# New places for all steps of a fused attention and feed-forward kernel, with a recalibrated planner

## The chip, the cores and the metric

The kernel runs on one core of a Trainium2 chip. The metric is the device time of one execution in microseconds, the median of several runs, lower is better. The engines are called as the profile calls them: PE is TensorE's matrix multiplication (PEld its weight loads), DVE is VectorE, ACT is ScalarE, POOL is GpSimd, and SP is SyncE, which here does nothing but issue transfers.

## The reference

Two stages, all in float32. The first is a linear recurrence for 4 batches and 8 heads over 768 time steps with head size 48; the second is a two-layer network on its output (3072 rows of 384 values, 2048 hidden).

```python
for t in range(S):
    cur = einsum('bhd,bhe->bhde', u * k[t], v[t])
    y[t] = einsum('bhd,bhde->bhe', r[t], state + cur)
    state = w[t][..., None] * state + einsum('bhd,bhe->bhde', k[t], v[t])
x = y.transpose(0, 2, 1, 3).reshape(B * S, H * D)
out = maximum(x @ w_in, 0) ** 2 @ w_out
```

## The kernel before, in words

**The work.** Time is cut into 6 chunks of 128 steps. For a chunk c and a batch b the *attention unit* (called A0.1 below for chunk 0, batch 1) loads r, k, w and v, turns r, k and w so that head and feature lie on the partitions, forms running products of w with a scan on DVE (L603, steps `scan`), scales r and k by them (`rt`, `rk`, `kn`), multiplies them on PE (`mt`, `mix`, L768 to L786), masks on DVE and writes the transposed output x, split into a high and a low part, as the operand of the network (`x`, L830). The recurrence's state goes from chunk to chunk: `dS` on PE (L760) is the new outer product, `S` on DVE (L847) adds it.

The network of a chunk (F0.5 is chunk 0, block 5 of 128 hidden units; 16 blocks) is `hp` on PE (nine matrix products, L869), squared ReLU and a split into two parts on ACT and DVE (steps `g`, L874 to L881), and `ob` on PE (three products for each of three output tiles, L888; L914 in the last chunk). Each product in float32 is made of three with split operands. The first blocks of chunk 0 (6) and of chunk 1 (8) are done in two halves, a for batches 0 and 1, b for batches 2 and 3, so that the network can start when half of the chunk's attention is there; after that every block takes 512 columns.

**Slices.** For chunk 0 the turning is done on PE (`turn`, L588). For later chunks it is done in two steps: DVE transposes 32 by 32 blocks (`z`, L542, two for a pair of batches), then 16 transfers that SP issues (`pt`, L552; 48 or 96 KB each, in pieces of 32 values) put the blocks into their places. The first scan of the chunk (L603) needs all 16. For the pair A1.0 and A1.1, SP can issue the first of them only when both `z` have ended.

**Weights.** W0 to W7 are the eight groups of both weight matrices. Of each, SP loads seven pieces: six of w_in (L468; 112 rows are 224 KB, 48 rows 96 KB, 32 rows 64 KB) and one of w_out (L470, 768 KB). Each half is then split into a high and a low part by ACT (widen, L487, and L507), three operations on DVE (L491, L495, L500) and one on POOL (L508). W3's pieces are wanted by block 6 of chunk 0, which comes after the halves.

**Order.** Every engine executes its instructions in order, and the order is written out by hand. Each step is registered with `P.add(engine, cost, rank, fn, ...)`, where rank is the next number of its row in the table `Places.PLACE`; `Plan.order` sorts each engine's steps by that number, so the numbers alone give the order on each engine. The planner then simulates the program with the costs given to `P.add` and the latencies `LAT`; from its times come three things only: the order in which the code of different engines is emitted, which buffer of a pool a step gets, and how many filler transposes PE executes while it waits (`P.filler`, L966: ten at the start, and up to as many as fit into a planned wait before 110 us). Steps marked `port` use a path to memory that DVE and POOL share, and the planner lets only one of them run at a time:

```python
t, news = max(s.ready, free.get(unit, 0.0), free.get("port", 0.0) if s.port else 0.0), {}
...
return None if s.todo or t == float("inf") else (t, unit)
...
at, unit = min(x for x in (start(u) for u, l in todo.items() if l) if x)
```

So among steps of several engines with one planned time the engine's name decides.

Of the kernel before, what the change touches and what calls it, by code (L numbers as in the profile page):

```python
# [9 lines left out]
F32 = mybir.dt.float32  # L10
# [4 lines left out]
AF = mybir.ActivationFunctionType  # L15
# [16 lines left out]
class Plan:  # L32
# [7 lines left out]
    LAT = {"pe": 0.2, "act": 0.1, "dve": 0.1, "pool": 0.1}  # L40
# [35 lines left out]
    def order(self):  # L76
# [89 lines left out]
class Places:  # L166
    PLACE = {
        "un": (39, 102, 107,),
        "load": (1, 3, 6, 2, 8, 11, 26, 19, 30, 34, 67, 86, 122, 136, 79, 340, 297, 317, 505, 499, 504, 707, 694, 700, 920, 906, 914, 1080, 1069, 1075, 1227, 1225, 1230, 1399,
# [4 lines left out]
        "turn": (9, 47, 50, 24, 29, 13, 35, 42, 65, 73, 78, 109, 113, 127,),  # L174
        "scan": (20, 16, 15, 18, 32, 28, 25, 27, 90, 72, 91, 87, 137, 124, 138, 123, 302, 326, 304, 329, 338, 324, 341, 342, 663, 598, 658, 656, 595, 590, 604, 586, 704, 762,
# [9 lines left out]
        "beta": (53, 59, 56, 61, 97, 103, 153, 177, 250, 357, 460, 447, 687, 685, 870, 863, 1074, 1063, 1162, 1161, 1304, 1336, 1494, 1489, 1680, 1617, 1809, 1859,),  # L185
        "flip": (251, 358, 461, 448, 670, 626, 879, 854, 1086, 1070, 1184, 1178, 1391, 1342, 1484, 1453, 1701, 1677, 1860, 1878,),
# [898 lines left out]
```

## Time and profile before

| | |
|---|---|
| time, median of 3 runs | 523.11 us (521.79 to 523.46) |
| the profiled execution: its own time | 520.64 us |
| its span, first to last instruction | 518.8 us |
| granted TensorE clock, mean | 0.995 of full speed |
| PE busy | 508.5 us (98%) |
| DVE, ACT, POOL busy | 361.5, 278.0, 106.6 us |

The trace is that of one execution. The time holds some 1.8 us around the span. L-numbers are lines of the kernel; "ob<-g,wo" means that the operation writes tile ob from tiles g and wo, and a bracket at the end of a timeline row is the idle time of that engine before it and what ended it.

### The profile page before, as it was taken

Reading aid. Unit: us, or ns where it says so; the run is one execution under the profiler, and the core shown is the slowest. Engines: PE = TensorE matmul, PEld = TensorE weight load, DVE = VectorE, ACT = ScalarE, POOL = GpSimd, SP = SyncE. Lnnn points to the kernel's source line nnn. Section 1 sums busy time; section 2 is a strip of 40 time slices with the busy share of each in tenths; the row PEclk is TensorE's granted clock in tenths of the full one; section 3 lists DMA queues with packets and bytes.
Section 4 is the critical chain, followed back from the end, with each engine's and each line's share of the span. In section 5 each row is a group of like instructions: output and inputs, shape, how many; then the busy total and the mean of one; then the engine's idle time right before and its main releaser. Section 6 shows DMA issues by size and latency. Waiting matters only on the chain.

```text
span 518.8 us, 12672 instructions
## 1 busy us (share of the span) xinstructions
PE 508.5 (98%) x4957; PEld 435.4 (84%) x4957; DVE 361.5 (70%) x723; ACT 278.0 (54%) x686; POOL 106.6 (21%) x141
## 2 busy tenths in 40 slices
PE   8999899999999999999999999999999999999996
PEld 7889798778999988888878788888888888889986
DVE  5999699998986878787878794846782342253323
ACT  4457679768936567636557354454562263223222
POOL 2355546235220413031050400220000000000000
PEclk9999989999999999999999999999999999999999
DMA  6899999776556566766646454345405001020001
GB/s 183 229 219 204 193 219 206 146 171 98 114 92 111 100 96 138 113 120 99 122 71 110 90 83 86 69 79 88 91 3 123 2 1 42 1 58 5 0 2 64
DMA packets 209186, 52.40 MB, mean 101 GB/s; under 512 B 200033, under 2 KB 204002, under 8 KB 209122
## 3 DMA queue, kind: packets, MB, share of 16 engines
q1 hardware_dynamic: 208802, 51.15, 51.8%
q8 instruction: 40, 0.66, 0.5%
q10 hardware_dynamic: 320, 0.40, 0.2%
q14 instruction: 24, 0.20, 0.1%
HBM read 33.03 MB, written 4.72 MB: 73 GB/s over the span
## 4 chain that ended last, share of the span: by engine, by line
PE 79%; SPq 14%; DMA 4%; issue 1%; DVE 1%; ACT 1%; DVEq 0%; ACTq 0%
PE ob L888 29%; PE a L869 20%; PE hp L869 13%; SPq L468 6%; PE ob L914 5%; SPq L552 4%; DMA ri<-in_moe_w_in_dram 2%; SPq L527 2%; PE a L786 2%; PE a L712 2%; PE hp L914 2%; PE a L753 1%; DMA pt<-st 1%; PE hp L786 1%; PE hp L712 1%
## 5 line engine op out<-in xcount | busy, mean ns | idle before, releaser
L888 PE MATMUL ob<-g,wo 128*128 128x512 f32 (+1 forms) x846 | 188.7, 365 | 2.7 <-DVE g L881 2.7
L888 PEld LDWEIGHTS ob<-g,wo 128*128 128x128 f32 x846 | 142.2, 190 | 27.7 <-DVE g L881 3.3
L869 PE MATMUL a<-x,wi 128*128 128x512 f32 (+1 forms) x594 | 132.6, 369 | 0.0
L869 PEld LDWEIGHTS a<-x,wi 128*128 128x128 f32 x594 | 103.0, 191 | 17.8 <-ACT g L880 0.2
L869 PE MATMUL hp<-x,wi 128*128 128x512 f32 (+1 forms) x396 | 86.3, 364 | 0.1
L869 PEld LDWEIGHTS hp<-x,wi 128*128 128x128 f32 x396 | 67.6, 189 | 12.3 <-DVE x L830 0.3
L874 ACT ACTIVATE t<-a 128x512 f32<-128x512 f32 (+1 forms) x66 | 36.0, 545 | 75.9 <-PE ob L888 34.1
L878 DVE SCALAR_TENSOR_TENSOR a<-a,t 128x512 f32<-128x512 f32 (+1 forms) x53 | 34.1, 643 | 52.4 <-ACT t L874 52.2
L874 ACT ACTIVATE t<-hp 128x512 f32<-128x512 f32 (+1 forms) x44 | 23.6, 537 | 54.2 <-PE hp L869 37.3
L881 DVE TENSOR_TENSOR g<-a,g 128x512 fp32r<-128x512 f32 (+1 forms) x66 | 40.7, 618 | 16.6 <-ACT g L880 16.1
L880 ACT CAST g<-a 128x512 fp32r<-128x512 f32 (+1 forms) x66 | 35.0, 532 | 28.8 <-DVE a L878 28.6
L878 DVE SCALAR_TENSOR_TENSOR hp<-hp,t 128x512 f32<-128x512 f32 (+1 forms) x35 | 22.6, 646 | 33.7 <-ACT t L874 33.5
L689 ACT ACTIVATE m<-near,beta 128x64 f32<-128x64 f32 x160 | 41.9, 338 | 2.4 <-PE hp L786 2.1
L603 DVE TENSOR_TENSOR_SCAN pt<-pt,zero 112x128 f32<-112x128 f32 x80 | 31.5, 422 | 10.6 <-DMA ri<-in_moe_w_in_dram 4.4
L632 POOL TENSOR_TENSOR st<-st 128x384 f32<-128x384 f32 x20 | 22.3, 1119 | 56.0 <-DVE st L542 53.9
L880 ACT CAST g<-hp 128x512 fp32r<-128x512 f32 (+1 forms) x44 | 23.1, 525 | 14.6 <-DVE hp L878 14.4
L881 DVE TENSOR_TENSOR g<-hp,g 128x512 fp32r<-128x512 f32 (+1 forms) x44 | 26.6, 605 | 4.1 <-ACT g L880 3.7
L914 PE MATMUL ob<-wo,g 128*128 128x384 f32 x144 | 28.7, 336 | 0.0
L542 DVE STREAM_TRANSPOSE st<-st 128x1152 f32<-128x1152 f32 x20 | 26.5, 1353 | 0.3 <-DMA st<-in_r_dram 0.3
L914 PEld LDWEIGHTS ob<-wo,g 128*128 128x128 f32 x144 | 25.6, 188 | 0.8
L634 POOL TENSOR_TENSOR st<-st,un 128x384 f32<-128x384 f32 x20 | 22.7, 1147 | 0.6
L508 POOL TENSOR_TENSOR wi<-q,wi 128x768 fp32r<-128x768 f32 x8 | 16.0, 1999 | 27.6 <-ACT wi L507 9.8
(166 smaller groups left out, 727.2 us busy)
## 6 DMA issues: line engine op xcount, KB each, us to landing
pt<-st SPq DMA_DIRECT2D x80, 96.0 KB, 2.7
ro<-in_moe_w_out_dram SPq DMA_DIRECT2D x8, 768.0 KB, 5.9
st<-in_r_dram SPq DMA_DIRECT2D x10, 384.0 KB, 5.2
st<-in_w_dram SPq DMA_DIRECT2D x10, 384.0 KB, 5.5
st<-in_k_dram SPq DMA_DIRECT2D x10, 384.0 KB, 4.7
pt<-st SPq DMA_DIRECT2D x80, 48.0 KB, 2.8
out_dram<-q SPq DMA_DIRECT2D x80, 48.0 KB, 1.9
ri<-in_moe_w_in_dram SPq DMA_DIRECT2D x16, 224.0 KB, 4.8
```

What stands on the lines that cost most here:

```text
L468: P.add("sp", 0.27 if i > KT else 0.0084 * n, rank("load_w"), lambda to=to, src=src: nc.sync.dma_start(out=to, in_=src), w=[("wi", g, i)], ...
L542: V.transpose(out=zt[:, i].rearrange("a t p q i -> a t (p q) i"), in_=sv[:, :, i].rearrange("s t p q x -> s t (p q) x"))
L603: lambda p=p: V.tensor_tensor_scan(out=pt[:, 0, p], data0=src(0)[:, p], data1=zero.broadcast_to([HP, C]), initial=1.0, op0=ALU.mult, op1=A ...
L634: P.add("pool", 1.0, rank("rk"), lambda: G.tensor_tensor(out=rk(), in0=rk(), in1=un.rearrange("s (h d) -> s h d", d=D), op=ALU.mult), r=[" ...
L689: A.activation(whole(Ms[j])[:, g, 1 - f], near, AF.Copy, scale=beta.tile[:, x:x + 1])
L869: T.matmul(hp.tile[:, 0:n], wi[f][:, wl, kt], xT[:, kt, xl, xs], start=(m == 0), stop=(m == 3 * KT - 1))
L874: P.add("act", 0.5 if full else 0.28, rank("g"), lambda: A.activation(t(), h(), AF.Relu), r=[hp], w=[(g, 1)])
L878: P.add("dve", 0.61 if full else 0.33, rank("g"), lambda: V.scalar_tensor_tensor(out=h(), in0=h(), scalar=0.0, in1=t(), op0=ALU.max, op1=A ...
L880: P.add("act", 0.53 if full else 0.31, rank("g"), lambda: A.copy(out=hi(), in_=h()), r=[hp], w=[(g, 0)])
L881: P.add("dve", 0.61 if full else 0.33, rank("g"), lambda: V.tensor_tensor(out=lo(), in0=h(), in1=hi().bitcast(F32), op=ALU.subtract), r=[h ...
L888: T.matmul(obs[kt][:, xs], wo[f][:, wl, kt], g.tile[0][:, gl, 0:n], start=(f == 0 and m == 0 and bs[0] == 0), stop=(f == NF - 1 and m == 2 ...
L914: T.matmul(obt()[:, 0:DM], g.tile[0][:, gl, o:o + C], wo[f][:, wl], start=(f == 0 and m == 0), stop=(f == NF - 1 and m == 2))
```

## The change

No instruction, tile or transfer is added, taken away or altered. Three things are: the table of places (all its numbers), the costs given for most kinds of step, with the latencies, and the planner's rule for the shared port: among steps with one planned time, the one that could have begun first without the port now goes first. The diff, cut to its core:

```diff
-    LAT = {"pe": 0.2, "act": 0.1, "dve": 0.1, "pool": 0.1}
+    LAT = {"pe": 0.25, "act": 0.14, "dve": 0.14, "pool": 0.15}
...
-            t, news = max(s.ready, free.get(unit, 0.0), free.get("port", 0.0) if s.port else 0.0), {}
+            asked, news = max(s.ready, free.get(unit, 0.0)), {}
+            t = max(asked, free.get("port", 0.0) if s.port else 0.0)
...
-            return None if s.todo or t == float("inf") else (t, unit)
+            return None if s.todo or t == float("inf") else (t, asked, unit)
...
-            at, unit = min(x for x in (start(u) for u, l in todo.items() if l) if x)
+            at, _, unit = min(x for x in (start(u) for u, l in todo.items() if l) if x)
...
-        "turn": (9, 47, 50, 24, 29, 13, 35, 42, 65, 73, 78, 109, 113, 127,),
+        "turn": (4, 17, 7, 10, 31, 1, 32, 40, 59, 62, 57, 117, 127, 121,),
...
-        "dS": (252, 257, 279, 275,),
+        "dS": (230, 205, 355, 246,),
...
-            P.add("act", 0.8, rank(nm), widen, r=parts, w=[q])
-            P.add("dve", 0.48, rank(nm), shift, w=[q], port=True)
+            P.add("act", 0.805, rank(nm), widen, r=parts, w=[q])
+            P.add("dve", 0.465, rank(nm), shift, w=[q], port=True)
...
-        P.add("pe", 0.67 if c else 0.915, rank("mt"), scores, r=RK + KK, w=mts, mode=3 if c else 1, claim=Ms)
+        P.add("pe", 0.67 if c else 1.06, rank("mt"), scores, r=RK + KK, w=mts, mode=3 if c else 1, claim=Ms)
...
-        P.add("act", 0.5 if full else 0.28, rank("g"), lambda: A.activation(t(), h(), AF.Relu), r=[hp], w=[(g, 1)])
+        P.add("act", 0.483 if full else 0.27, rank("g"), lambda: A.activation(t(), h(), AF.Relu), r=[hp], w=[(g, 1)])
```

The other costs are changed in the same manner, nearly all of them down by a few per cent. Of the new table this is what the steps below speak of. The place on the engine counts its steps from 0.

| step | engine | number before, after | place on the engine before, after |
|---|---|---|---|
| A0.0 x, A0.1 x (second part) | DVE | 139, 163 to 204, 203 | 43, 50 to 47, 46 |
| the two masks of A0.2 | DVE | 181, 176 to 217, 213 | 54, 53 to 50, 49 |
| the two z of A1.0 | DVE | 184, 191 to 229, 235 | 55, 56 to 53, 55 |
| first of the 16 slices of A1.0 | SP | 198 to 183 | 48 to 49 |
| last of the 16 slices of A1.0 | SP | 274 to 249 | 66 to 68 |
| scans of A1.0 and A1.1 ahead of the next network g | DVE | two (302, 304) to four (317, 319, 324, 325) | 82, 83 to 81 to 84 |
| that g | DVE | F0.0b g 313 to F0.5a g 327 | 85 to 86 |
| the ob that needs that g | PE | F0.0b ob(0) 320 to F0.5a ob(1) 292 | 67 to 66 |
| A0.2 dS | PE | 279 to 355 | 56 to 73 |
| F0.0b hp | PE | 295 to 259 | 61 to 58 |
| W3's last two pieces of w_in | SP | 167, 203 to 212, 216 | 45, 49 to 57, 59 |
| W3's w_out | SP | 241 to 228 | 59 to 64 |

On SP three pieces of weights come to stand ahead of the last slice that stood behind it (W5's 112 rows, W5's 48 rows and W7's 48 rows: 224, 96 and 96 KB), and one (32 rows of W5, 64 KB) goes from before the slices to behind them. Between the first and the last slice inclusive SP issues 19 transfers before and 20 after. The w_out load of W3 has seven of the slices behind it before and four after.

Over the whole program 464 of PE's 576 steps get another place on PE (2.0 places on average, 19 at most), 580 of DVE's 684 (3.9), 439 of SP's 467 (9.7, 62 at most). The first 101, 105, 117 and 127 steps of PE are the same steps before and after, in another order. PE changes 39 times into the tiled mode of the attention's small products and back before, 40 times after. At the end SP has the first store of the last chunk, two stores of the chunk before it and the last store, where before the two went ahead of both.

## Rows read from the trace of the kernel before

**Rows 1.** The page: busy time and share of the span; the chain of waits by engine.

```profile
PE 508.5 (98%) x4957; PEld 435.4 (84%) x4957; DVE 361.5 (70%) x723; ACT 278.0 (54%) x686; POOL 106.6 (21%) x141
...
PE 79%; SPq 14%; DMA 4%; issue 1%; DVE 1%; ACT 1%; DVEq 0%; ACTq 0%
```

**Rows 2.** Busy time by stretch; after the comma: granted clock, DMA share, GB/s.

```profile
40.00:45.00 5.00, 5.00 (x48) 4.51 (x46) 5.00 (x7) 4.60 (x12) 1.96 (x4) 1.00 1.04 253
50.00:55.00 5.00, 5.00 (x83) 4.33 (x83) 4.98 (x8) 3.99 (x11) 4.81 (x3) 1.00 0.78 168
...
70.00:110.00 40.00, 39.47 (x409) 33.47 (x409) 38.27 (x64) 31.77 (x73) 18.59 (x15) 1.00 0.96 187
110.00:310.00 200.00, 200.00 (x2231) 170.02 (x2230) 166.57 (x358) 123.81 (x346) 49.77 (x69) 1.00 0.60 106
310.00:510.00 200.00, 200.00 (x1397) 169.09 (x1396) 95.47 (x186) 80.84 (x176) 6.43 (x9) 1.00 0.22 43
```

**Rows 3.** Timeline of PE, 60.5 to 67 us: start, length, line, operation, [idle before].

```profile
61.64 1.12 PE L888 MATMUL ob<-g,wo 128*128 128x256 f32 x8
65.44 1.91 PE L888 MATMUL ob<-g,wo 128*128 128x256 f32 x12 [2.68 <-DVE g L881]
```

**Rows 4.** Timeline of DVE, 57 to 66 us.

```profile
58.49 0.55 DVE L491 TENSOR_SCALAR q<-q 128x768 uint32<-128x768 uint32 x1
63.46 0.74 DVE L603 TENSOR_TENSOR_SCAN pt<-pt,zero 112x128 f32<-112x128 f32 x2 [4.42 <-DMA ri<-in_moe_w_in_dram]
64.11 0.93 DVE L495 SCALAR_TENSOR_TENSOR q<-ro,q 128x768 uint32<-128x768 uint32 x1
64.97 0.42 DVE L881 TENSOR_TENSOR g<-hp,g 128x256 fp32r<-128x256 f32 x1
```

**Rows 5.** The chain of waits, 36 to 66 us: start, length, what.

```profile
45.40 1.72 SPq L552
...
56.54 0.62 SPq L552
...
57.20 5.87 DMA pt<-st
```

**Rows 6.** Busy time by stretch around the half clock.

```profile
67.00:68.00 1.00, 1.00 (x6) 1.00 (x6) 1.00 (x3) 1.00 (x3) 0.00 (x0) 0.50 1.03 185
...
69.00:70.00 1.00, 1.00 (x7) 1.00 (x6) 1.00 (x2) 0.85 (x3) 1.00 (x1) 0.50 1.43 206
```

**Rows 7.** Timeline of DVE, 35 to 43.5 us: the first chunk's x, the block transposes.

```profile
36.08 0.55 DVE L830 SCALAR_TENSOR_TENSOR x<-hp,x 128x384 fp32r<-128x384 f32 x1
...
39.80 2.62 DVE L542 STREAM_TRANSPOSE st<-st 128x1152 f32<-128x1152 f32 x2
```

**Rows 8.** Timeline of SP, 40 to 58 us, around the first slice.

```profile
40.77 0.38 SPq L470 DMA_DIRECT2D ro<-in_moe_w_out_dram  x1
42.57 0.71 SPq L552 DMA_DIRECT2D pt<-st  x1
```

**Rows 9.** DMA of the stretch 42 to 57.8 us: packets, by size.

```profile
DMA packets 8207, 2.99 MB, mean 189 GB/s; under 512 B 7464, under 2 KB 7464, under 8 KB 8204
```

**Rows 10.** Timeline of PE, 53.5 to 57 us: two dS products.

```profile
54.80 1.13 PE L760 MATMUL a<-v,m 128*64 128x48 f32 x32
```

**Rows 11.** Timeline of PE, 89.5 to 91 us.

```profile
89.99 0.71 PE L966 MATMUL a<-ident 128*128 128x128 f32 x5
90.46 0.72 PE L869 MATMUL hp<-x,wi 128*128 128x512 f32 x2
```

**Rows 12.** Timeline of PE, 95.8 to 96.8 us.

```profile
96.14 0.49 PE L966 MATMUL hp<-ident 128*128 128x128 f32 x3
96.39 0.70 PE L888 MATMUL ob<-g,wo 128*128 128x512 f32 x2
```

**Rows 13.** Timeline of SP, 508 to 519 us.

```profile
513.32 1.92 SPq L927 DMA_DIRECT2D out_dram<-m  x2
```

**Rows 14.** Timeline of ACT, 511 to 519 us.

```profile
515.32 0.37 ACTq L927 DMA_DIRECT2D out_dram<-m  x1
```

More of the change, by code (lines that the diff above doesn't have):

```diff
@@ L266 @@
-        "far": (705, 719, 633, 647, 956, 958, 881, 897, 1106, 1138, 1095, 1118, 1216, 1231, 1212, 1232, 1418, 1419, 1365, 1371, 1528, 1538, 1493, 1540, 1835, 1837, 1790, 1834,
-            2030, 2032, 1970, 1979,),
-        "again": (2035, 2078,),
-        "late": (1983, 2128, 2075, 2076,),
-        "flag": (2224, 2354, 2362,),
+        "un": (19, 91, 87,),
+        "load": (8, 11, 12, 2, 18, 14, 38, 45, 39, 72, 28, 66, 108, 116, 51, 278, 274, 308, 503, 510, 504, 691, 696, 683, 870, 866, 867, 1056, 1048, 1065, 1207, 1218, 1208,
[4 rows of a table added]
@@ new lines @@
+        "turn": (4, 17, 7, 10, 31, 1, 32, 40, 59, 62, 57, 117, 127, 121,),
+        "scan": (27, 26, 25, 16, 13, 9, 5, 22, 142, 102, 139, 118, 176, 159, 177, 173, 317, 341, 349, 324, 319, 359, 325, 336, 632, 581, 687, 656, 568, 575, 577, 597, 740,
[9 rows of a table added]
+        "beta": (42, 65, 48, 63, 74, 77, 138, 146, 262, 384, 514, 525, 728, 710, 930, 932, 1064, 1036, 1166, 1167, 1361, 1359, 1561, 1518, 1677, 1721, 1832, 1861,),
+        "flip": (267, 371, 536, 590, 669, 652, 911, 918, 1076, 1058, 1144, 1164, 1330, 1319, 1565, 1464, 1672, 1720, 1825, 1932,),
[5 rows of a table added]
@@ L271 @@
+        "far": (684, 713, 679, 694, 955, 959, 927, 940, 1125, 1130, 1099, 1131, 1156, 1186, 1198, 1213, 1383, 1398, 1412, 1413, 1591, 1598, 1514, 1589, 1718, 1723, 1780, 1811,
+            1879, 2197, 2115, 2130,),
+        "again": (1997, 2156,),
+        "late": (1966, 1992, 2094, 2150,),
+        "flag": (2292, 2357, 2361,),
     }
@@ L440 @@
     rows = Slot("a")
-    P.add("pe", 0.75, PLACE("un"), lambda: T.matmul(rows.tile[:, 0:H * D], ones, un, start=True, stop=True), r=["un"], w=[rows])
+    P.add("pe", 0.65, PLACE("un"), lambda: T.matmul(rows.tile[:, 0:H * D], ones, un, start=True, stop=True), r=["un"], w=[rows])
     P.add("act", 0.45, PLACE("un"), lambda: A.activation(un, rows.tile[:, 0:H * D], AF.Copy, scale=-1.0), r=[rows], w=["un"])
@@ L501, in low @@
                                        op0=ALU.logical_shift_right, op1=ALU.bitwise_or)
[L503 to L508 removed]
+            P.add("act", 0.805, rank(nm), widen, r=parts, w=[q])
+            P.add("dve", 0.465, rank(nm), shift, w=[q], port=True)
+            P.add("dve", 0.865, rank(nm), sign, r=parts, w=[q], port=True)
+            P.add("dve", 0.865, rank(nm), low, r=parts, w=[q], port=True)
+            P.add("act", 0.725, rank(nm), lambda q=q, tt=tt, part=part, to=place_: A.copy(out=to(tt[:, 0]), in_=part(q.tile)), r=[q], w=parts + [lead])
+            P.add("pool", 1.83, rank(nm), lambda q=q, tt=tt, part=part, to=place_: G.tensor_tensor(out=to(tt[:, 1]), in0=part(q.tile), in1=to(tt[:, 0].bitcast(F32)), op=ALU.subtract),
                   r=[q, lead], w=[(nm, g, "rest")])
@@ L545, in attention @@
                 for i in range(2):
-                    d["z"] = P.add("dve", 1.3, rank("z"), lambda i=i: blocks(i), r=[(st, i, x) for x in range(3)], w=[(z, i)])
+                    d["z"] = P.add("dve", 1.27, rank("z"), lambda i=i: blocks(i), r=[(st, i, x) for x in range(3)], w=[(z, i)])
                 used = [s for s in P.steps if any(type(x) is tuple and x[:2] == ("pt", n % 2) for x in s.keys)]
@@ L588, in turn @@
                             T.matmul(to[j * J:j * J + n, :, :, y], rows[:, y * D:y * D + n], pick[:, :, j], start=True, stop=True, skip_group_check=True)
-                turned = P.add("pe", 0.94, rank("turn"), turn, r=[(st, ui, i)], w=[ps[i]], mode=3)
+                turned = P.add("pe", 0.93, rank("turn"), turn, r=[(st, ui, i)], w=[ps[i]], mode=3)
                 if b == 0 and i == 0:
@@ L601, in attention @@
         for p in range(NP):
-            P.add("dve", 0.32, rank("scan"),
+            P.add("dve", 0.315, rank("scan"),
                   lambda p=p: V.tensor_tensor_scan(out=pt[:, 0, p], data0=src(0)[:, p], data1=zero.broadcast_to([HP, C]),
@@ L657, in attention @@
         KK = EK if c else [PT[2]]
[L658 removed]
+        P.add("dve", 0.67 if c else 0.595, rank("kn"), scaled, r=[y0] + keys(2), w=KK, port=c > 0)
         Ms = [Slot("m") for j in range(2)]
@@ L682, in weigh @@
                     G.tensor_tensor(out=to, in0=heads, in1=by, op=ALU.mult)
-            P.add("pool", 1.5, rank("bv"), weigh, r=[vt, beta], w=[bv])
+            P.add("pool", 1.28, rank("bv"), weigh, r=[vt, beta], w=[bv])
         for j in range(2) if c else ():
@@ L729, in attention @@
             P.add("pe", 0.32, rank("ktp"), ktok, r=KK, w=[ktp], claim=[Kt])
-            P.add("act", 0.44, rank("kt"), lambda: A.copy(out=kv(Kt), in_=kv(ktp)), r=[ktp], w=[Kt])
+            P.add("act", 0.425, rank("kt"), lambda: A.copy(out=kv(Kt), in_=kv(ktp)), r=[ktp], w=[Kt])
             if c:
@@ L804, in attention @@
             P.add("pe", 0.35, rank("bonus"), bonus, r=[bv], w=[yb, (yb, 3)])
-            P.add("pe", 0.35, rank("mix"), part([SPLIT]), r=[vt, *Ms], w=[(yb, 3)], mode=3)
-            P.add("act", 0.2, rank("mix"), lambda: A.copy(out=ly.tile, in_=ybv()[0:HP, KT]), r=[(yb, 3)], w=[ly])
+            P.add("pe", 0.22, rank("mix"), part([SPLIT]), r=[vt, *Ms], w=[(yb, 3)], mode=3)
+            P.add("act", 0.15, rank("mix"), lambda: A.copy(out=ly.tile, in_=ybv()[0:HP, KT]), r=[(yb, 3)], w=[ly])
             P.add("pe", 1.6, rank("mix"), between, r=[vt, *Ms, ly], w=[yb], mode=3)
-            outs = [("x", yb, lambda: ybv()[:, 0:KT], lambda: xT[:, :, 0, cs], lambda: xT[:, :, 1, cs], xk + (0,), 0.4, 0.47)]
+            outs = [("x", yb, lambda: ybv()[:, 0:KT], lambda: xT[:, :, 0, cs], lambda: xT[:, :, 1, cs], xk + (0,), 0.37, 0.455)]
         else:
@@ L842, in attention @@
             if c == 0:
-                P.add("pe", 0.443, rank("dS"), outer, r=[vt, Kt], w=[dS], mode=3)
+                P.add("pe", 0.4, rank("dS"), outer, r=[vt, Kt], w=[dS], mode=3)
             Sd = Ss[b][:, PC:].rearrange("a (p e) -> a p e", p=NP)
@@ L898, in back @@
                                         in_=obs[kt][:, 2 * i * C:2 * i * C + 2 * C].rearrange("p (y i) -> p y i", i=IR))
-                        P.add("dve", 0.38, rank("os"), back, r=[("ob", kt, i)], w=[(os_, kt)])
+                        P.add("dve", 0.37, rank("os"), back, r=[("ob", kt, i)], w=[(os_, kt)])
                     for b in range(2 * i, 2 * i + 2):
```

102 lines of the change are left out of this document (46 added, 56 removed), and 146 rows, old and new, of the table PLACE.

## The prediction

> **What bounds the kernel now.** I read the page first: PE is busy for 98% of the span and the chain of waits runs through it for 79% [rows 1]. Nothing that only fills idle time of other engines can bring much; the question is where PE's missing 10 us lie. The busy time by stretch answers that [rows 2]: from 110 to 510 us PE is busy for the whole 400 us, at full clock. There a new order has nothing to win, and could only lose by opening a wait. What can be won lies ahead of 110 us.
>
> There PE has one large wait: it stops three products into an `ob` and resumes at 65.44 us after 2.68 us without work [rows 3] (F0.0b ob(0)). It waits for a g on DVE, and DVE shows why: after its last operation at 58.49 us it stands idle for 4.42 us, then does two scans at 63.46, a weight split at 64.11 and only then the g at 64.97 [rows 4]. The g was late because it is queued behind the scans of chunk 1, and these wait for the last of A1.0's slices. The profile puts the idle time down to a weight load; I go by the chain instead, which ends in a slice issued at 57.20 us that needs 5.87 us to land, at 63.07 [rows 5]. Soon after the stall the granted clock is down at 0.50, the lower of its two levels (1.2 instead of 2.4 GHz), in stretches at 67 and 69 us [rows 6]; with its neighbours that is about 3.3 us, so some 1.65 us of work are lost to it. Between 70 and 110 us PE is idle for another 0.53 us [rows 2], and fillers hide 0.47 us of waiting at 90 us [rows 11] and 0.25 us at 96 us [rows 12]: 1.25 us in all. Stall, half clock and these come to some 5.6 us, the most that is to be had here; the rest of the 10 us lies at the start and at the end of the span.
>
> **The change, part by part.** Nothing computes less or more, and the planner's rule, costs and latencies reach the chip only through buffers, emission order and fillers; no price of their own: 0. What acts is the order on the engines.
>
> *A, earlier start.* DVE does the x of batches 0 and 1, on which the network's start hangs, at places 47 and 46 instead of 43 and 50; the second stands at 36.08 us [rows 7]. Summing the durations of what is ahead of the later of them, about 1.9 us less stands there. PE's network so starts earlier, but it reaches the same stall, and whoever arrives earlier at a gate waits longer: 0. What counts is when the gate opens.
>
> *B, the last slice.* The first `z` starts at 39.80 us [rows 7], right behind the masks, and SP, free after the 0.38 us at 40.77, can issue the first slice at 42.57 [rows 8]. In the new order the two masks are still ahead of `z`, but two of the other operations are not, and about 1.4 us less work stands ahead of the second `z`; SP has about 41.6 us as its earliest, since it has one issue more ahead. The first slice so starts up to 0.95 us sooner. Against that, 20 issues instead of 19 from the first to the last slice cost 0.62 us [rows 5]: sum −0.3 us, if SP's issuing sets the pace. If the transfers set it, 352 KB more (224 + 96 + 96 − 64) lie ahead of the last slice; at the 253 GB/s of the stretch 40 to 45 us they take 1.4 us [rows 2]. Both speak: one issue of a slice is held for 1.72 us instead of 0.62 [rows 5], so the queue is full at times, and yet the DMA share is only 0.78 between 50 and 55 us [rows 2], which leaves 1.1 us free for 1.4 us of bytes that are now sent earlier. I take the difference and round it up, +0.4, with −0.3 and +1.4 as ends.
>
> In this stretch 7464 of 8207 packets are under 512 bytes and the DMA moves 189 GB/s [rows 9], while the weight pieces go in longer packets. The Trainium skill ("DMA: Bandwidth & Descriptors", Specifications) gives 512 bytes as the least for line rate and about 358 GB/s as the limit from memory for one core; as an estimate from that page the 352 KB would take 1.0 us, which the free 1.1 us would swallow, and the sum below would come out 0.4 us lower. No row here shows the rate of the weight pieces alone.
>
> *C, four scans ahead of the g.* The next g stands behind four scans and the split instead of two scans and the split. Two scans take 0.65 us start to start [rows 4]: +0.65, with 0 as the lower end if the other scans come later than the data.
>
> *D, a product moved behind the stall.* A0.2's dS goes from place 56 to 73 on PE. Two dS take 1.13 us [rows 10], one 0.57, with its own switch of mode 0.6: work that PE did while it would have waited anyway is now done after: +0.6.
>
> *E, later waits.* B, C and D leave PE 1.65 us later at about 68 us. The waits at 70 to 110 us are for other engines; DVE itself is shifted only by B. So they shrink as PE comes later, by up to their 1.25 us: −1.25, with 0 as the other end.
>
> *F, half clock.* The stall stays, so I let the stretch come again: 0, between −1.65 if it is gone and +1.65 if it comes twice.
>
> *G, one more change of mode* on PE: no row shows its price alone; it lies between 0 and half of a dS (0.3), and as it leaves no idle time in the rows of the pair I take the lower part, +0.1.
>
> *H, the tail.* Two stores of chunk 4 now stand on SP between the first and the last store of chunk 5. The two that it issues now take 1.92 us from 513.32, the wait between them included [rows 13]; two more at some 0.6 us each put the last issue at about 515.2 to 516, beside ACT's last store at 515.32 [rows 14]. It becomes about equally late: +0.1, bounds 0 and 0.5.
>
> Sum: 0 + 0.4 + 0.65 + 0.6 − 1.25 + 0 + 0.1 + 0.1 = +0.6 us. The profiled execution took 520.64 us, 2.47 less than the median of the runs; I apply the difference to the median: 523.11 + 0.6 = 523.7. What a measurement of this kernel can tell from no change is about 0.3%, 1.6 us.
>
> **The rivals.**
>
> *Faster: the gate opens earlier.* If slices are issued from 41.6 us and SP is never held, 20 issues at 0.66 us end at 54.8 and the last lands between 58 and 61 us. Scans then start up to 2.7 us earlier, PE follows, the stall closes and with it the half clock goes (−1.65): −4.5 at the far end, 518.6; half of the gain without the stall's end gives 521. For it: the DMA share of 0.78 [rows 2], and that the first chunk's loads and the loads of A1.0 stand earlier on SP. Against it: the held issues and the 5.87 us of the last slice [rows 5]. It decides from a last slice landing before 61 us.
>
> *Slower: the gate opens later and the later waits don't give it back.* The bytes set the pace (+1.4), DVE is then late by as much, and every wait behind it moves along, so E is 0: 1.4 + 0.65 + 0.6 + 0.2 = +2.9, 526.0. A longer stall can also bring a second half-clock stretch, +1.65: 527.6. For it: W3's w_out now stands five places later with only four slices behind it, and two W3 splits stand ahead of the scans on DVE, so the gate has a second bolt; and W3's last two pieces of w_in stand among the slices, with the x of A0.3, which F0.0b hp needs, behind W3's split. Against it: DVE was idle for 4.42 us there [rows 4], which can cover a split of 0.9 us. It decides from scans that start after 65 us.
>
> Before the stretch at 0.50 PE had stood idle in the stall [rows 3, 6]. The Trainium skill ("TensorE: Matmul & The Clock Gate", Part 1) says that idleness throttles PE and activity releases it; a longer stall would by that rule bring the stretch back for certain, and a closed one would free the clock. That is the last term of both rivals.
>
> *No effect.* The table could be, for PE, the old order: its first 101, 105, 117 and 127 steps are the same sets, moved by 2 places on average. Then the time is 523.1.
>
> **How the numbers follow.** Forecast with its small terms 0.33, no effect 0.05: both within 0.3% (0.38). Faster 0.32, slower 0.30: the single place that decides can move either way by the bounds of B. The forecast's own range is 523.0 (B at −0.3) to 526.0 (B at +1.4 and E at 0), its upper end already the rival's. The range for 8 in 10 reaches to the middle of the faster case, 519.6, and past the slower one's first price to 526.6; beyond them about 0.1 is left on either side.
>
> **What would show it.** Right: PE still has one wait of 2 to 5 us for a g of L881, now in F0.5a's ob, the first scan of chunk 1 starts at 63.5 to 64.3 us with four scans ahead of that g, and 110 to 510 us stays full. A is right if the first hp starts before 35.5 us and time is not shorter by it. Wrong: the first scan before 61 us (faster), the first scan after 65 us, or a second wait of PE over 1 us (slower), or any idle time of PE behind 110 us, for which I have set no price.

## The result, and the profile after

The changed kernel takes 530.46 us (median of 6 runs, 525.73 to 531.5), the kernel before 522.25 us on the same chip (6 runs, 521.32 to 523.46): the ratio is 1.0135 with a 95% interval of 1.0093 to 1.0178. It is slower by about 7 us by this ratio (the two medians are 8.2 us apart), outside the predicted range of 519.6 to 526.6. The profiled execution took 531.5 us, 529.5 of them the span; against the profile of before (518.8) that is 10.7 us more, so the two profiles together show rather more than the medians do. Line numbers of the changed kernel are those of before plus 1; in some kernels of the experiments they stand up to 8 further (the kn of L657 is L664 or L665 there).

The page after: busy time, and the chain of waits by engine, to be held against [rows 1].

```profile
PE 513.3 (97%) x4949; PEld 438.1 (83%) x4949; DVE 362.9 (69%) x723; ACT 275.7 (52%) x686; POOL 110.1 (21%) x141
...
PE 76%; SPq 13%; DVE 3%; DMA 3%; ACT 2%; issue 2%; POOL 1%; ACTq 0%; DVEq 0%; POOLq 0%
```

PE's busy time rose by 4.8 us although no work was added, which points to its clock, and DVE's part of the chain from 1% to 3%. The windows say where. After the comma: busy time of PE, PEld, DVE, ACT and POOL, then granted clock, DMA share, GB/s.

```profile
70.00:100.00 30.00, 30.00 (x255) 25.51 (x256) 26.75 (x44) 27.01 (x58) 15.18 (x10) 1.00 0.89 183
100.00:110.00 10.00, 8.44 (x166) 7.02 (x156) 7.95 (x17) 4.13 (x12) 3.37 (x4) 0.83 0.97 213
...
120.00:130.00 10.00, 7.45 (x64) 6.19 (x64) 9.53 (x9) 8.41 (x19) 7.52 (x7) 0.94 0.65 93
130.00:140.00 10.00, 10.00 (x50) 8.21 (x45) 6.65 (x16) 4.95 (x19) 0.00 (x0) 0.72 0.75 144
110.00:310.00 200.00, 195.69 (x2196) 166.17 (x2195) 161.42 (x338) 121.26 (x342) 47.90 (x67) 0.98 0.57 100
310.00:510.00 200.00, 200.00 (x1392) 168.20 (x1391) 103.35 (x207) 80.97 (x181) 10.18 (x13) 1.00 0.25 47
```

Where before had PE busy for all of the 200 us from 110 to 310 [rows 2], 4.31 us are now missing, and 1.56 us between 100 and 110, where before missed 0.53. The timeline of PE gives the places. One row each of: the first chunk's turning, the network's start, the ob that the prediction's g releases (this row takes in a few products ahead of it), the hp at 90 us, and four resumptions after a wait.

```profile
20.67 1.00 PE L589 MATMUL a<-perm,st 128*64 128x64 f32 x28 [1.91 <-DMA st<-in_k_dram]
...
38.43 1.33 PE L870 MATMUL a<-x,wi 128*128 128x256 f32 x9
...
66.08 1.70 PE L889 MATMUL ob<-g,wo 128*128 128x256 f32 x12
...
90.56 1.78 PE L870 MATMUL a<-x,wi 128*128 128x512 f32 x7
...
104.81 0.25 PE L769 MATMUL hp<-v,m 64*64 64x48 f32 x2 [1.51 <-DVE m L721]
...
129.03 0.47 PE L713 MATMUL a<-pt 48*64 48x128 f32 x1 [2.56 <-DVE pt L657]
...
161.25 0.98 PE L889 MATMUL ob<-g,wo 128*128 128x256 f32 x6 [0.87 <-DVE q L898]
...
275.47 1.88 PE L870 MATMUL a<-x,wi 128*128 128x512 f32 x7 [0.89 <-DVE x L831]
```

Up to 100 us nothing is lost: the hp of F0.8 starts at 90.56 instead of 90.46 [rows 11], and A1.0's `mt` at 99.00 instead of 99.02. Then the same steps of PE start later and later than before: A1.1's `mix` by 2.6 us, A1.2's next product by 8.7 (140.68 against 131.99), chunk 1's ob by 9.8 (168.57 against 158.75), A4.1's `mix` by 10.6 (306.36 against 295.76), and there it stays to the end.

Four waits of PE come to 1.51 + 2.56 + 0.87 + 0.89 = 5.8 us. The rest is the clock. Behind the first two waits PE is granted 0.50, the lower level of 1.2 GHz:

```profile
105.00:106.00 1.00, 1.00 (x40) 1.00 (x37) 1.00 (x5) 0.20 (x1) 0.00 (x0) 0.50 1.26 256
...
134.00:135.00 1.00, 1.00 (x4) 0.81 (x4) 0.00 (x0) 0.53 (x1) 0.00 (x0) 0.50 1.12 228
```

These stretches run from 105 to 108.4 and from 128.9 to 135.7 us, 10.2 us in all, in which 5.1 us of work are lost. Waits and clock together, 10.9 us, less the 0.5 us by which PE waited there before, are 10.4 of the 10.6 us lost.

What made PE wait is seen on DVE. First the DVE rows around 103, 124 and 160 us, then POOL's.

```profile
102.48 1.79 DVE L604 TENSOR_TENSOR_SCAN pt<-pt,zero 112x128 f32<-112x128 f32 x1 [0.68 <-issue]
104.20 0.56 DVE L721 COPY_PREDICATED m<-caus,hp 128x384 f32<-128x384 uint8 x1
...
122.90 0.69 DVE L882 TENSOR_TENSOR g<-hp,g 128x512 fp32r<-128x512 f32 x1 [0.35 <-ACT g L881]
123.50 5.47 DVE L657 TENSOR_TENSOR pt<-pt,m 112x256 f32<-112x256 f32 x2
...
159.24 0.59 DVE L721 COPY_PREDICATED m<-caus,hp 128x384 f32<-128x384 uint8 x1 [0.58 <-PE hp L713]
...
160.41 0.78 DVE L898 STREAM_TRANSPOSE q<-ob 128x256 f32<-128x256 f32 x2 [0.58 <-PE ob L889]
```

```profile
102.15 1.84 POOL L509 TENSOR_TENSOR wi<-q,wi 128x768 fp32r<-128x768 f32 x1 [6.05 <-ACT wi L508]
...
121.82 1.87 POOL L509 TENSOR_TENSOR wo<-q,wo 128x768 fp32r<-128x768 f32 x1 [5.76 <-ACT wo L508]
123.62 0.39 POOL L620 COPY Ec<-pt 112x4 f32<-112x4 f32 x1
123.98 1.01 POOL L633 TENSOR_TENSOR st<-st 128x384 f32<-128x384 f32 x1
124.96 1.01 POOL L635 TENSOR_TENSOR st<-st,un 128x384 f32<-128x384 f32 x1
125.94 1.80 POOL L509 TENSOR_TENSOR wo<-q,wo 128x768 fp32r<-128x768 f32 x1
127.69 1.00 POOL L635 TENSOR_TENSOR st<-st,un 128x384 f32<-128x384 f32 x1
128.65 0.69 POOL L852 TENSOR_TENSOR S<-S,Ec 112x192 f32<-112x192 f32 x1
```

*At 103 us.* The first scan of A1.3 has moved from behind to ahead of the two masks of A1.0 (places 143 to 137 on DVE). It waits for its data (the last slice was issued at 97.93 us and took some 4.3 to land) and then takes 1.79 us instead of the 0.40 of a later one, beside a weight split on POOL that ends at 103.99, 0.3 us before the scan does. PE waits for the first of the two masks, which begins at 104.20; before, both were begun by 102.61.

*At 124 us.* The last `kn` of A1.3 (L657, two halves) has moved behind three g. Its second half starts at 123.89 and ends at 128.97: 5.08 us, where the median of that line is 0.42. All the while POOL does one operation after the other, on the port that the two engines share; `kn` ends 0.28 us behind the last product of POOL's chain (127.69 + 1.00 = 128.69). Before, the same `kn` met the same chain of POOL and lost little:

```profile
118.15 2.63 DVE L656 TENSOR_TENSOR pt<-pt,m 112x256 f32<-112x256 f32 x2
```

```profile
117.49 1.86 POOL L508 TENSOR_TENSOR wo<-q,wo 128x768 fp32r<-128x768 f32 x1 [4.77 <-ACT wo L507]
119.31 1.19 POOL L632 TENSOR_TENSOR st<-st 128x384 f32<-128x384 f32 x1
120.47 2.28 POOL L634 TENSOR_TENSOR st<-st,un 128x384 f32<-128x384 f32 x2
122.71 1.85 POOL L508 TENSOR_TENSOR wo<-q,wo 128x768 fp32r<-128x768 f32 x1
124.51 0.19 POOL L619 COPY Ec<-pt 112x4 f32<-112x4 f32 x1
```

There it took 1.48 and 1.23 us, and POOL's products 1.2 instead of 1.0: the two engines took turns. Besides `kn`, the head of POOL's chain differs: the copy of A1.2's Ec (112 x 4 values) stood behind the chain and now stands directly ahead of it. The last of the three products has also moved behind the second split.

*At 160 us.* A mask of A2.1 (159.24 us), which itself waits for PE, now stands ahead of two output transposes of chunk 0 (160.41); before, the transposes stood ahead of the mask. PE's ob needs the transposes done and waits 0.87 us.

### The profile page after: what moved, and what is told of

Same layout as the page of the kernel before. It is cut to its first block, busy times and chain, and to the rows that moved or that the text cites. A ratio compares the mean times of both kernels' runs of the same rounds, so it can differ in the third digit from the quotient of the medians.

```text
span 529.5 us, 12648 instructions
## 1 busy us (share of the span) xinstructions
PE 513.3 (97%) x4949; PEld 438.1 (83%) x4949; DVE 362.9 (69%) x723; ACT 275.7 (52%) x686; POOL 110.1 (21%) x141
## 4 chain that ended last, share of the span: by engine, by line
PE 76%; SPq 13%; DVE 3%; DMA 3%; ACT 2%; issue 2%; POOL 1%; ACTq 0%; DVEq 0%; POOLq 0%
PE ob L889 28%; PE a L870 18%; PE hp L870 14%; SPq L469 6%; PE ob L915 5%; SPq L553 4%; PE a L787 2%; PE a L713 2%; PE a L915 2%; DMA ri<-in_moe_w_in_dram 2%; SPq L528 1%; SPq L471 1%; PE a L754 1%; PE hp L787 1%; DMA v<-in_v_dram 1%
## 5 line engine op out<-in xcount | busy, mean ns | idle before, releaser
L889 PE MATMUL ob<-g,wo 128*128 128x512 f32 (+1 forms) x846 | 191.0, 367 | 0.9 <-DVE q L898 0.9
L870 PE MATMUL a<-x,wi 128*128 128x512 f32 (+1 forms) x585 | 126.0, 361 | 0.9 <-DVE x L831 0.9
L870 PEld LDWEIGHTS a<-x,wi 128*128 128x128 f32 x585 | 98.8, 188 | 18.1 <-DVE x L831 1.3
L870 PE MATMUL hp<-x,wi 128*128 128x512 f32 (+1 forms) x405 | 91.7, 371 | 0.0
L870 PEld LDWEIGHTS hp<-x,wi 128*128 128x128 f32 x405 | 70.6, 188 | 12.8
L879 DVE SCALAR_TENSOR_TENSOR a<-a,t 128x512 f32<-128x512 f32 (+1 forms) x51 | 32.5, 637 | 42.2 <-ACT t L875 42.0
L882 DVE TENSOR_TENSOR g<-a,g 128x512 fp32r<-128x512 f32 (+1 forms) x65 | 38.9, 605 | 15.8 <-ACT g L881 15.6
L879 DVE SCALAR_TENSOR_TENSOR hp<-hp,t 128x512 f32<-128x512 f32 (+1 forms) x37 | 24.3, 656 | 32.9 <-ACT t L875 32.8
L882 DVE TENSOR_TENSOR g<-hp,g 128x512 fp32r<-128x512 f32 (+1 forms) x45 | 28.3, 628 | 19.0 <-ACT g L881 18.8
L733 POOL MEMSET pt<- 32x512 f32 x16 | 8.1, 518 | 76.0 <-PE a L713 29.9
```

Source lines behind the costliest of these rows:

```text
L870: T.matmul(hp.tile[:, 0:n], wi[f][:, wl, kt], xT[:, kt, xl, xs], start=(m == 0), stop=(m == 3 * KT - 1))
L879: P.add("dve", 0.595 if full else 0.325, rank("g"), lambda: V.scalar_tensor_tensor(out=h(), in0=h(), scalar=0.0, in1=t(), op0=ALU.max, op1 ...
L882: P.add("dve", 0.595 if full else 0.325, rank("g"), lambda: V.tensor_tensor(out=lo(), in0=h(), in1=hi().bitcast(F32), op=ALU.subtract), r= ...
L889: T.matmul(obs[kt][:, xs], wo[f][:, wl, kt], g.tile[0][:, gl, 0:n], start=(f == 0 and m == 0 and bs[0] == 0), stop=(f == NF - 1 and m == 2 ...
```

## The experiments

The theory after the first look: the loss is in the table, at these three places, and most of it in what DVE does at 124 us. The rivals: the planner (its rule and costs change buffers, emission and fillers), the order of the first 90 us, and many small shifts rather than three. All numbers given as ratios are against the kernel before on the same chip, with 95% intervals. In the diffs a step is followed by its number; the numbers are only exchanged among the steps shown.

**Planner or table.** The old table with the new planner:

```diff
-    LAT = {"pe": 0.2, "act": 0.1, "dve": 0.1, "pool": 0.1}
+    LAT = {"pe": 0.25, "act": 0.14, "dve": 0.14, "pool": 0.15}
...
-            at, unit = min(x for x in (start(u) for u, l in todo.items() if l) if x)
+            at, _, unit = min(x for x in (start(u) for u, l in todo.items() if l) if x)
```

> The old table of places with the new costs, latencies and port rule. Queue theory (the loss comes from the new order on DVE, behind 100 us): every engine's order is the old one, so the time is that of before, 520.7 to 523.8 us, and PE shows no wait over 1 us behind 100 us. Planner theory (the new costs and the new rule give other buffers and fewer fillers, and those make the loss): slower than before by 4 us or more. Clock theory (the loss is half clock that comes by chance): the same as before in PE's waits, with half-clock stretches in some executions.

522.75 us, 0.9984 (0.9959 to 1.0009). And the reverse, the new table with the old costs, latencies and rule:

```diff
-            at, _, unit = min(x for x in (start(u) for u, l in todo.items() if l) if x)
+            at, unit = min(x for x in (start(u) for u, l in todo.items() if l) if x)
```

> The new table with the old costs, latencies and port rule. Queue theory: the order alone makes the loss, 528 to 532 us with the waits at 103 and 126 us. Planner theory: without the new costs the new order would be at 523 to 526 us.

529.78 us, 1.0141 (1.0079 to 1.0203), with the long `kn` again (5.09 us) and a wait of 2.6. The wait at 103 us is not in this profile, against the expectation; instead PE waits 1.1 us at 44 us and 1.9 us at 59. So the loss comes with the table, and the planner does nothing to the time that can be told from noise.

**The early part.** The new order up to number 460 (about 90 us), the old one behind it:

```diff
-order: new numbers throughout
+order: new numbers up to 460, behind it all steps in their old order
```

> All engines in the new order up to number 460 (some 90 us on PE) and in the old order after that, with the new planner. Queue theory: the new order costs nothing up to there (PE was 0.1 us behind at 90 us in the changed kernel's profile), and the old order behind it has none of the three waits: 521.5 to 524 us, within 0.3% of the kernel before or a little better. If the early part has its own loss that only shows later (buffers, weights that come later): over 525 us.

522.61 us, 0.9992 (0.996 to 1.0025). All that the prediction reckoned with in the first 90 us, taken together, cannot be told from nothing.

**DVE's stretch.** The 55 steps of DVE between about 96 and 137 us in their old order, 46 numbers exchanged:

```diff
-DVE, 96 to 137 us: new order
+DVE, 96 to 137 us: old order, all else new
```

> The changed kernel with the 55 steps of DVE between about 96 and 137 us in the order that they had before, everything else as changed. Queue theory: this stretch of one engine holds nearly the whole loss, 522.5 to 525.5 us. If PE's, SP's or POOL's new order makes the loss, it stays over 528 us; if all share it, it lies between.

524.48 us, 1.0059 (1.0015 to 1.0103): this stretch of this one engine holds a good part of the loss, about half by the ratios (1.0135 to 1.0059; the intervals are too wide to say how much). Some stays, since DVE's old order now meets the other engines' new one; PE waits 1.4 us for another operation of it.

**The place at 103 us**, the masks ahead of the scan again:

```diff
-A1.3 scan(0) 568, A1.0 mask(0) 569, A1.0 mask(1) 574
+A1.0 mask(0) 568, A1.0 mask(1) 569, A1.3 scan(0) 574
```

> The changed kernel, but on DVE A1.3's first scan goes behind the two masks of A1.0 instead of ahead of them. Queue theory: the masks no longer wait for the last slice, PE's wait of 1.5 us at 103 us shrinks to under 0.5 and the half clock behind it goes; the wait at 126 us stays. Time 2 to 3.5 us less than the changed kernel's 530.5, so 527 to 528.5 us. Planner theory and clock theory: no change, 528 to 531 us, with the wait at 103 us still there.

527.89 us, 1.0091 (1.0054 to 1.0128). The wait at 103 us is gone from the profile, the one for `kn` stays at 2.6 us with its 5.08 us on DVE. The ratio fell by 0.4%, which the intervals do not tell from nothing; shown is that the move takes this wait away.

**The place at 124 us, by DVE**, `kn` ahead of the three g again:

```diff
-three g 689, 690, 697, A1.3 kn 698
+A1.3 kn 689, the three g 690, 697, 698
```

> The changed kernel, but on DVE the last product of A1.3 (kn, two operations that need the shared port) goes ahead of three g of the network. Queue theory: it runs before POOL begins its chain of five operations, the 5.1 us that one of its halves takes become about 0.4, and PE's wait of 2.6 us at 126 us goes with the half clock behind it: 2.5 to 6 us less than the changed kernel, 524.5 to 528 us; the wait at 103 us stays. If the long operation is long by itself and not by the port, it stays at some 5 us and the time at 528 to 531 us.

526.91 us, 1.0063 (1.0032 to 1.0094). DVE's timeline:

```profile
118.43 0.74 DVE L664 TENSOR_TENSOR pt<-pt,m 112x256 f32<-112x256 f32 x2
...
120.88 5.43 DVE L622 TENSOR_TENSOR pt<-pt 112x508 f32<-112x508 f32 x1
```

`kn` takes its normal 0.74 us for both halves, but the next operation of DVE that uses the port, the `rt` of A1.2, now takes 5.43. The wait is handed on: it belongs to whoever comes to the port at that moment, not to `kn`. It cost PE 1.2 us instead of 2.6, as less hangs on `rt`.

Both edits together:

```diff
+the edits of the masks and of kn
```

> Both moves together. Queue theory: they add up, 5 to 9 us less than the changed kernel, 521.5 to 525.5 us; what is left over the kernel before are the two waits of 0.9 us at 160 and 275 us. If a wait that is taken away only comes back at the next place in the queue, the sum is less than half of that, over 526 us.

525.19 us, 1.0032 (1.0004 to 1.006), `rt` 5.92 us, a wait of 1.7. Then `rt` also put behind A1.3's masks:

```diff
-A1.3 mask(0) 701, mask(1) 702 behind A1.2 rt 699
+A1.3 mask(0) 699, mask(1) 701, A1.2 rt 702
```

> Both moves of before, and the next operation on DVE that needs the shared port (A1.2's rt, which took 5.4 and 5.9 us once kn was out of the way) goes behind the two masks of A1.3 that PE waits for. Queue theory: PE's wait of 1.2 to 1.7 us at 127 us goes; 1 to 2 us less than both moves alone, 523 to 524.5 us, that is within 0.3% of the kernel before. If the long operation is no cause of that wait: no change, 525 to 526 us.

524.89 us, 1.005 (1.002 to 1.0081). The wait is gone from the profile, but no gain can be told from the run before: a miss.

**POOL's part.** If DVE waits until POOL comes to a stop, more work on POOL must prolong the wait. The split of W7's last piece done twice (it writes the same values):

```diff
-G.tensor_tensor(out=to(tt[:, 1]), in0=part(q.tile), ...)
+[G.tensor_tensor(out=to(tt[:, 1]), in0=part(q.tile), ...) for _ in range(1 + twice)]
```

> The changed kernel with POOL's last operation on W7's w_out done twice (the second writes the same values once more): one operation of 1.8 us more in POOL's chain at 124 to 129 us. Port theory (DVE's operation gets the port only when POOL's chain of operations ends): DVE's long operation grows from 5.1 to 6.9 us, PE's wait at 126 us from 2.6 to some 4.4, and the time by 1.5 to 3.5 us to 532 to 534 us. If the operation is long by itself or for its data, it stays at 5.1 us and the time at 530.5.

526.88 us, 1.0095 (1.0064 to 1.0126): a miss, and a useful one. DVE's row and POOL's:

```profile
120.75 4.51 DVE L657 TENSOR_TENSOR pt<-pt,m 112x256 f32<-112x256 f32 x2
```

```profile
120.88 0.38 POOL L620 COPY Ec<-pt 112x4 f32<-112x4 f32 x1
...
123.17 3.79 POOL L509 TENSOR_TENSOR wo<-q,wo 128x768 fp32r<-128x768 f32 x2
```

`kn` was done sooner, at 125.25, within 0.3 us of the point where the second of the two equal splits began (125.05). So DVE doesn't simply wait until POOL has nothing left; there are points in POOL's chain at which it gets the port and others at which it doesn't.

**The copy ahead of the chain.** Only POOL's order is changed, A1.2's Ec behind the chain as before:

```diff
-POOL: A1.2 Ec 641, product 643, product 649, W7 split 650, product 672
+POOL: product 641, product 643, W7 split 649, product 650, A1.2 Ec 672
```

> The changed kernel with one step of POOL back at its old place: A1.2's small copy (Ec) goes behind the chain of two products, the weight split and a product instead of ahead of it. Port theory as it stands after the run with POOL's operation done twice (DVE gets the port only where POOL leaves a gap, and the chain that follows the copy has none): the chain stays, so DVE's long operation stays at 3 to 5 us and the time at 528 to 531. Copy theory (DVE loses its turns only in a chain that begins with the copy; elsewhere it mostly gets the port after one operation of POOL): the long operation falls to 1 to 1.5 us, PE's wait of 2.6 us at 126 us to under 1, and the time to 526.5 to 528.5 us.

524.75 us, 1.0035 (1.0002 to 1.0068), against 1.0135 with the copy ahead: one step of 112 x 4 values on an engine that is 21% busy is worth about 1% of the kernel. The time fell below the 526.5 to 528.5 us that the copy theory had expected: the direction was right, the size was not. DVE's order is untouched; its rows, and POOL's:

```profile
120.99 1.62 DVE L664 TENSOR_TENSOR pt<-pt,m 112x256 f32<-112x256 f32 x2
122.53 1.49 DVE L622 TENSOR_TENSOR pt<-pt 112x508 f32<-112x508 f32 x1
```

```profile
121.13 1.20 POOL L640 TENSOR_TENSOR st<-st 128x384 f32<-128x384 f32 x1
122.29 1.19 POOL L642 TENSOR_TENSOR st<-st,un 128x384 f32<-128x384 f32 x1
123.44 2.30 POOL L516 TENSOR_TENSOR wo<-q,wo 128x768 fp32r<-128x768 f32 x1
```

The engines take turns as before the change, and PE's wait is gone. The rival was that it is the order (Ec early, and what it releases) and not the copy on the port. So to this kernel a second copy of the same size was added, directly ahead of the chain, of constants into a tile that nobody reads:

```diff
-lambda: G.tensor_tensor(out=rk(), in0=rk(), in1=vals(2), op=ALU.mult)
+lambda: [G.tensor_copy(out=tiny, in_=ut[:, :, 0:1]) if (c, b) == (2, 0) else None,
+         G.tensor_tensor(out=rk(), in0=rk(), in1=vals(2), op=ALU.mult)]
```

> The changed kernel with Ec moved back (524.75 us), and another small copy of 112x4 values, of constants and with nobody who reads it, on POOL directly ahead of the same chain of products. Copy theory (a copy as such ahead of the chain lets POOL keep the port): DVE's operation is long again, 4 to 5 us, PE waits 2 to 2.6 us for it, and the time is 527 to 531 us. If it was Ec's own place or its data (it reads what DVE scans), the time stays at 524 to 525.5 and the operations at 1.2 to 1.5 us.

529.86 us, 1.0159 (1.0136 to 1.0182): all of it back.

```profile
122.04 5.45 DVE L665 TENSOR_TENSOR pt<-pt,m 112x256 f32<-112x256 f32 x2
```

```profile
122.16 0.38 POOL L641 COPY tiny<-ut 112x4 f32<-112x4 f32 x1
122.50 1.01 POOL L641 TENSOR_TENSOR st<-st 128x384 f32<-128x384 f32 x1
```

The second half of `kn` again takes 5.07 us and PE waits 2.5 for it. So it is neither Ec's data nor what Ec releases: a copy of the same size that has nothing to do with either does it too.

**The place at 160 us.** To the kernel with masks, `kn` and `rt` moved, the two output transposes ahead of the mask:

```diff
-A2.1 mask(1) 883, os(1,0) 884, os(1,1) 899
+os(1,0) 883, os(1,1) 884, A2.1 mask(1) 899
```

> The three moves on DVE that removed the waits at 103 and 126 us, and two transposes of the output (L898, the second half of chunk 0) ahead of a mask of A2.1 that waits for PE. Queue theory: PE's wait of 0.9 us at 150 to 160 us goes, 0.5 to 1 us less than the three moves alone (524.9): 523.9 to 524.4 us. If the wait is for something else than the place of the transposes: 524.9.

525.06 us, 1.0014 (0.9976 to 1.0051): a miss in the absolute time, and too wide an interval to tell. The wait of 0.9 us is gone; a new one of 2.1 us for a g at 120 us stands in its profile. There `kn`, now ahead of that g, met a weight split on POOL that ended at 121.49 us; its second half ended at 121.77, and the g stood behind it.

**All three, each by its own single move**: Ec behind the chain, the masks ahead of the scan, the transposes ahead of the mask.

```diff
+the edits of the Ec copy, of the masks and of the transposes (11 numbers)
```

> Three single moves in the changed kernel: POOL's copy Ec back behind the chain, A1.3's first scan behind the two masks of A1.0, the two output transposes ahead of the mask of A2.1. Queue and copy theory: each takes away one wait of PE (2.6, 1.5 and 0.9 us) and brings none, so 1.5 to 2.5 us less than the copy's move alone (524.75): 522 to 523.5 us, within 0.3% of the kernel before, and PE without a wait over 0.6 us behind 100 us. If the waits only wander, 524.5 us or more.

521.72 us, 0.9998 (0.9978 to 1.0019). PE's waits from 95 us to the end, with the total, the count and the longest:

```profile
PE a L877 <- DVE x L838: 0.4, 1, 0.4
PE a L794 <- DVE junk L825: 0.3, 1, 0.3
```

All the other numbers are the change's, and the loss is gone. The three moves together explain it, to within the 0.2% of the interval; what each is worth by itself the intervals do not resolve (1.0035 with the copy's move alone, 0.9998 with all three). The rest of the new order is worth nothing that can be measured, and no version was measurably faster than the kernel before.

## Why the prediction was wrong

The likeliest case had the direction right (+0.6 us), but its size and its place were wrong. The slower rival was right in direction only, and that by luck: its prices (526.0 and 527.6 us) were too low, and its condition, scans behind 65 us, did not hold, as they started at 64.08. One of its signs did come, a second wait of PE over 1 us, but 40 us later and from another cause.

**What failed** is the sentence that from 110 to 510 us a new order "could only lose by opening a wait", left without a price. The prediction named this as its blind spot ("any idle time of PE behind 110 us, for which I have set no price"). It gave its terms up to 110 us to one gate at 63 us, and none to the DVE steps that had moved behind it. What the runs showed in its place: 4.31 us of idle PE between 110 and 310 us, with 6.8 us at half clock behind the longest of these waits, and 1.56 us idle with 3.4 us at half clock just ahead of 110. They come from places at which a step that PE needs had come to stand behind one that waits, and three moves take the loss away.

The zero for the planner's rule, costs and latencies held (both exchanges of planner and table). But the prediction has no term at all for the places of POOL's and DVE's port operations against each other, though [rows 2] show POOL busy for 49.77 us between 110 and 310; this order made the longest of the waits, 2.56 us.

**Term by term:** DVE's rows around the gate come first.

```profile
64.08 1.36 DVE L604 TENSOR_TENSOR_SCAN pt<-pt,zero 112x128 f32<-112x128 f32 x4
...
66.22 0.74 DVE L882 TENSOR_TENSOR g<-a,g 128x256 fp32r<-128x256 f32 x2
```

Then two rows of SP: the wait of the w_out load ahead of the slices, and the first slice.

```profile
41.30 3.02 SPq L471 DMA_DIRECT2D ro<-in_moe_w_out_dram  x1
...
44.93 5.92 SPq L553 DMA_DIRECT2D pt<-st  x8
```

- *A, earlier start: wrong.* The first hp starts at 38.43 us, 1.8 later than before (36.67); the test was "before 35.5". PE had waited 1.91 us for the load of k at 20.67, but that is not the whole reason: in the profiles of the other kernels with the new early order this wait is 0.2 to 1.7 us where it is named, and the first hp starts at 37.2 to 38.4 us, later than before in each, even where the wait is 0.2. What else delays it is open.
- *B, the last slice: close in size, by luck.* The scans start 0.62 us later than in [rows 4]; +0.4 was taken, ends −0.3 and +1.4. But the first slice was issued at 44.93 us instead of 42.57, 2.4 us later, where up to 0.95 sooner was expected: a w_out load ahead of it was held on SP for 3.02 us. The last slice was issued at 59.14 instead of 57.20 and landed after 4.6 us instead of 5.87, at 63.77, 0.7 us later than before. The two misses cancelled in part.
- *C, four scans ahead of the g: right.* The g is at 66.22 instead of 64.97, 1.25 later, which is B's 0.62 and about 0.63 more; +0.65 was taken.
- *The stall itself: wrong.* It was to stay with 2 to 5 us. PE came there later, by small waits (1.91 us at 20 us among them), and so found the g ready: the ob at 66.08 has no idle time before it. D thus cannot be seen by itself.
- *E, the later waits: wrong in sign.* They were to shrink by 1.25 us between 70 and 110 us; PE's idle time there grew from 0.53 to 1.56 us, with the half clock at 105 us on top. That the lag at 90 us was +0.1 us, near the +0.4 of A to E, is luck: the stall and its half clock were gone, and PE had been busy for 54.2 us of the first 60 instead of 56.8.
- *F, half clock: wrong.* It let stall and stretch come again. Both are gone together, which fits the tie that the prediction made between them; two other stretches, three times as long (10.2 us against 3.3), came behind the new waits.
- *G and H:* at the end 10.7 us are missing, at 296 us 10.6; H was taken at +0.1.

On the clock, the prediction weighed a sentence of the Trainium skill ("TensorE: Matmul & The Clock Gate", Part 1), that idleness throttles PE and activity releases it. It bore out here in its direction: no stall at 63 us, no half clock at 67; a wait of 2.56 us, then the longest stretch at 0.50. It is not certain for each wait, though: in the kernel with the added copy, PE waited 1.5 and 2.5 us at the same two places, and the clock stayed up, as in this window behind the second one (its clock is the 1.00 ahead of the last two numbers).

```profile
130.00:132.00 2.00, 2.00 (x13) 1.70 (x12) 1.69 (x5) 1.38 (x5) 0.00 (x0) 1.00 0.58 100
```

So the 10.7 us of the profile are one execution's; what the clock adds differs from run to run (its mean was 0.989 to 1.000 in the six runs). How much of the difference to the 7 us of the ratio this makes up is not known: over the six runs the clock and the span do not go together (0.997 with a span of 528.6 us, 1.000 with 525.5).

## What to carry to other kernels

When an order is changed everywhere, the places where PE has no wait are not safe: go through each engine's moved steps and ask whether a step that PE needs soon has come to stand behind one that waits (here a mask behind a scan that waited for data, and transposes behind a mask that waited for PE). Where two engines share a port, look at their orders together. At one place of this kernel a short operation at the head of POOL's chain made DVE's step wait for most of the chain; look at such a place in a trace before you trust an order there. To find such a loss, lay the start times of the same PE steps side by side in both profiles: here three of the four jumps of this lag named the three moves, and undoing them, eleven numbers of over 2000, brought everything back. The fourth, behind the wait of 0.89 us at 275 us, needed no move of its own: with the three undone that wait was 0.4 us.

## What was not expected of the hardware

**Who gets the shared port.** The change's planner lets the one who asked first go first. The chip doesn't: `kn` stood ready at 123.89 us, and POOL began four more operations (123.98, 124.96, 125.94, 127.69) before it got through. The Trainium skill ("SBUF — State Buffer", SBUF: two separate sides) says that the port pair is an exclusive lock, held for a whole instruction, and that whichever starts first gets it; who gets it next when both want it, that section doesn't say. The traces agree with the first: each time DVE was let in, it was at the end of one of POOL's operations. On the second they show that it can go either way. In seven profiles (the changed kernel, the reverse exchange of planner and table, the kernels with the masks, with `kn`, with both, with the doubled split and with the added copy) the short copy stood directly ahead of POOL's chain and DVE had a port operation ready beside it: it was passed over at three or more ends in a row and held for 4.1 to 5.9 us. In five (the kernel before, the old table with the new planner, the early part alone, Ec moved back, all three moves) no copy stood there, and DVE was let in at the next end each time, after 1.2 to 2.1 us.

That a short copy ahead of the chain makes the difference is shown, by moving it away and by adding another. Why is open. It isn't the mere lateness of DVE's request (0.12 us before the copy's end), as far as the traces go: at other places requests 0.2 to 0.45 us before the end of a product were served at that end. And it isn't the copy alone: at 277 us of the changed kernel DVE was passed over once between two equal products, and in the kernel with the doubled split it was let in between the two splits. Nor do copy and moment together settle it: in the kernel with the added copy the very next operation on DVE, the `rt`, asked 0.12 us before the end of the Ec copy and was let in at that end, done after 0.68 us, though POOL's next product stood behind the copy:

```profile
127.42 0.68 DVE L623 TENSOR_TENSOR pt<-pt 112x508 f32<-112x508 f32 x1
```

```profile
127.14 0.40 POOL L628 COPY Ec<-pt 112x4 f32<-112x4 f32 x1
```

In all seven profiles DVE's request fell while the copy ran, 0.12 to 0.16 us before its end; in the three that remain (DVE's old stretch, `rt` moved too, the transposes moved too) the copy stood ahead of the chain but no request fell there. No run varied the moment of the request or the copy's length on purpose.
